# Sliding-window attention and a token mixer on one core: q and k in two-token rows, loads by four heads, mixing products with 128 columns, a new emission table

## The chip, the cores and the metric

The kernel runs on one core of a Trainium2 chip. Five engines matter: PE (TensorE, matrix products and transposes), ACT (ScalarE), DVE (VectorE), POOL (GpSimd, which here does little but issue the loads) and SP (SyncE, which issues the stores). Loads and stores themselves are moved by the core's 16 DMA engines. Results of PE go to PSUM, which has 8 banks; everything else lies in SBUF, with 128 partitions. The metric is the device time of one execution in microseconds (us), lower is better.

## The reference

Inputs are q, k and v of shape (8 batches, 8 heads, 576 tokens, 64), and three weights. Attention is causal within a window of 128 tokens, with a linear bias per head; its output, as rows of 512 numbers per token, goes into a mixer over the tokens of a batch.

```python
scores = scale * np.matmul(q, k.transpose(0, 1, 3, 2))      # scale 1/8
mask = (rel >= 0) & (rel < window)                           # rel = query - key, window 128
scores = np.where(mask, scores + bias[None], -1000000000.0)
attn = softmax(scores)
x = (attn @ v) as (batch, token, 512)
wq, wk = x @ w_q, x @ w_k                                    # 64 columns each
mixed = (1/8 * wq @ wk.T) @ x                                # per batch
out = np.maximum(mixed, 0.0) @ w_out
```

## The kernel before, in words

The kernel first makes a list of operations (`plan.op`), batch by batch, and then emits them in an order that is written out in the string `ORDER`. An entry such as `228P4+1` or `407G` means: operation 228 on PE with its result in PSUM bank 4, after 1 padding matmul on zeros; operation 407 on POOL. The letters are P for PE, A for ACT, D for DVE, G for POOL, S for SP. Every engine executes its own entries strictly in that order. An entry that has to wait holds all entries of the same engine behind it. The costs, due times and the `mode` that are passed to `plan.op` play no part in the emission; only the table does. `plan.run` (L117) checks that no operation stands ahead of one that it depends on. Before, the table has 773 entries, 279 of them on PE and 118 loads on POOL.

Per batch:

- **Loads** (`load`, L230, profile line L234; `load_qk` L237, `load_v` L266). All loads are issued by POOL and turn fp32 into fp16 on the way. Batches 0 and 1 take q and k in rows of six tokens (1536 B), two heads at a time, 192 rows per load (`ldsix`). Batches in `PAIRED` (2 and 3) take q and k in rows of two tokens (512 B), 1024 rows per load, that is 256 tokens of all eight heads. The others take rows of one token (256 B), 1024 rows for 128 tokens. v comes in rows of one token, 1024 rows per load (`ldv`); batch 0 takes it by heads, 512 rows per load. The last 64 tokens of each batch come in loads of their own (`ldqkt` into the tile `ntl`, `ldvt`), 512 rows on 64 partitions.
- **Buffers.** q and k lie in `natq` and `natk`, three buffers each (`NN`); v in `vn`, three (`NV`). So the loads of batch b wait until PE has transposed q and k of batch b-3, and used v of batch b-3.
- **Transposes of q and k** on PE (`q_transposes`): L378 for six-token rows, L407 for two-token rows (16 transposes of 128x64 per step), L418 for one-token rows (8 of 128x128), L435 for the last 64 tokens. Each step is copied to `qkT` by ACT (L222) or DVE (L224). For two-token rows the copy also puts the tokens back in order.
- **Attention** (`unit`, `values`): scores L483 in 64x64 tiles, exp on ACT (L496), the bias as a product with a table on DVE (L500), values L526 in 128x128 and 64x64 tiles, reciprocal and normalisation on DVE (L554, L555), transposes of the result L572.
- **Mixing** (`mixing`, `mix_one`, `outputs`): L608 (wk), L637 (wq), L650 (their product with x, `gm`), the mixing products L673 with the relu at L622 or L624, the output product L703 (four matmuls of 512 columns), a copy to `osb` and a store by SP (L710). There are 36 such output steps.

The mixing product is, before, four 64x64 matmuls of 288 columns per step j: two row halves c of `gm` and `wqT`, and two column halves y, each into its own 64 partitions of PSUM.

The order of loads on POOL is not batch by batch. The table mixes loads of up to three batches, and puts each load wherever its buffer is free and its use is not yet near.

Of the kernel before, what the change touches and what calls it, by code (L numbers as in the profile page):

```python
# [15 lines left out]
D = 64  # L16
H = 8
# [14 lines left out]
0G 1D 2A 4G 3D 5G 21D 31G 6D 32G 22A 20D 7D 33G 24A 34G 39G 40G 23D 12A 48P0+8 41G 14A 8A 50P1+2 42G 15A 51D 18A  # L32
43G 52P2+2 9A 16D 11A 35G 10D 17A 54P3+2 36G 49A 53D 55A 37G 64P4+3 19D 65A 38G 70P6 13D 67P0 44G 68A 66D 45G
71A 69D 46G 56P2+8 47G 73P4 72D 57A 58P3 25G 78P0 59D 74P 26G 60P6 75D 83P2 130G 61A 62P7 84A 131G 79P 132G 76P6
80D 63A 133G 77A 86P4+1 85D 89P2 138G 87A 81P7 139G 82D 90A 88D 140G 92P0+5 91D 143P6 141G 93P 144A 145P4 94D
142G 97P2 146A 98P 134G 159P6 99D 95P5 160A 135G 149P4 147P0 96D 136G 150A 100P1 148D 137G 101A 161D 162P2+2 27G
102P6 163A 28G 104P7 103D 164D 106P5 105A 29G 165P0 107A 108D 166A 30G 168P2 169P 109A 167D 231G 151P4 116P6
170D 114P0 152A 229G 153P5 115A 117D 171P4 154A 234G 155P2 172A 178P0 156D 110P6 230G 157P3 179A 173P4 158D 228G
111A 174P 112P0 180D 184P2 113A 235G 175D 232G 181P6+3 185A 121P0 233G 182A 127P1 186D 236G 122D 124P4 128A 183D
123S 176P5 129S 125A 187P2 238G 177D 243P6 126S 188P 320G 244A 192P0 189D 249P7 239G 247P4 250A 190P5 248D 193P  # L40
118P6 237G 194D 241P2 240G 119A 191D 195P3 242A 120S 318G 245P7 196D 246D 197P4 317G 251P0 198A 254P2 319G 252A
273P6 201P5 414G 255A 253D 332P4 324G 204D 199P0 274A 256D 323G 257P2 333D 202A 270P6 258A 407G 275D 271A
276P2+3 259D 322G 277A 260P6+2 272D 261P 203D 200A 265P2 278D 325G 205P4 207P0 262D 266P 206A 208A 328P4 267D
408G 326P5 329A 211P6 209P0 327D 284P2 212A 502G 330P4 210D 285P 331A 412G 263P6 286D 268P7 213P5 321G 264A 269A
287P0 405G 214A 340P2 288D 353P6 341A 215S 403G 337P4 334P0 354A 342D 225P2 409G 335A 355D 219P3 226D 338A 410G
279P6 216P0 336D 227S 220A 339D 404G 280P 221S 217A 356P4 281D 359P2 357A 218S 222P1 406G 360A 282P0 499G 358D
343P6 348P4 283D 415G 344P 361D 289P2 413G 345D 349P 290A 291P3 411G 350D 420P0 292A 293P2 416G 223D 421A 426P6
224S 294D 296A 295D 497G 428P7 427A 297P4 301P0 429D 299P2 302A 417G 346P6 300D 351P7 298A 367P0 352D 362P2 347A
419G 368P 363P 369D 303P4 422P7 418G 304A 364D 370P6 500G 311P4 371A 423D 507G 424P5 312A 305P0 589G 425D 313S
365P1 496G 306A 430P2 366D 511P6 431A 307S 498G 372P7 512D 449P4 503G 373A 432D 433P0 450A 452P2 376P6 501G 453A  # L50
374P7 451D 314P4 506G 377D 434A 454D 308P5 315D 594G 375A 379A 435D 513P2 316S 458P0 587G 309D 514A 459P 378D
310S 439P4 460D 504G 384P6 382P2 440P 385A 383D 461P0 508G 380P6 462D 386P2 381A 441D 436P0 586G 387A 509P6 437A
391P7 510D 505G 394P2 438D 392D 600G 515P3 395A 444P4 393S 516D 397P0 396S 597G 596G 536P6 398D 445P 537A 520P2
446D 595G 399S 605P1 521A 442P0 592G 606D 517P6 539P4 518A 538D 523P2 682G 447P1 522D 540A 542P6 519D 588G 543A
448D 455P4+2 541D 400P1 591G 456A 544D 526P6 401D 524A 593G 527P 457D 545P4 402S 388P1 601G 443A 528D 463P2 679G
389A 525D 546P 464P 390S 590G 547D 529P0 531P6 530A 607P1 690G 465D 532P 608A 548P4 598G 533D 466P5 603P0 599G
467A 550P2 549D 604A 534P1 468P6 602G 535D 551P 469A 684G 611P7 552D 472P5 612A 680G 470P4 473D 475A 474D 553P1
471A 683G 554A 478P2 482P6 476P4 479D 483A 555P0 686G 477D 609P1 556A 480P2 610D 559P6 687G 481D 616P4 681G 562A
632P0 617A 560D 613P2 561D 493P7 688G 633A 618D 619P4 494D 685G 614A 487P6 634D 495S 620A 635P0 689G 615D 638P2
557P7 488D 639A 691G 694P4 621D 489S 490P5 636A 640D 695D 627P2 558A 622P0 491A 637D 563P6 628P 492S 564A 698P4  # L60
629D 623P 699A 565P6 484P5 624D 566A 692P2 485A 641P0 693A 567P6 486S 642P 569P4 625P3 643D 570A 696P2 626A
646P4 697D 644P0 568A 647P 645D 703P2 648D 700P6 704A 574P1 701A 649P0 705D 577P4 575D 725P2 702D 578A 576S
706P6 571P5 726A 650D 579S 709P0 707A 727D 630P4 710P 722P2 631A 711D 719P6 723A 651P4 708D 712P0 720A 653P1
724D 714P2 652A 713D 733P6 572A 721D 715P 654A 573S 655P4 716D 734P 657A 728P0 656A 735D 717P5 658A 729P 718A
661P2 583P4 730D 662A 736P6 584A 731P7 737D 665P2 659P0 732D 585S 663P4 666A 580P6 660D 664A 738P7 581D 673P2
739A 582S 742P3 674A 740P0 675S 744D 745A 743A 670P1 741D 746P4 749P6 671A 755P2 748D 667P0 756A 757D 672S 747A
751A 752P2 750A 668D 676P1 753A 754A 669S 758P4 677A 767P5 678S 759A 761P6 760S 768D 764P7 762D 769S 770P0 763S
765A 766S 771A 772S
# [90 lines left out]
NN = 3  # L159
NV = 3  # L160
VHEADS = (0,)
PAIRED = (2,3)
# [5 lines left out]
def kernel(  # L168
# [10 lines left out]
    nc = tc.nc  # L179
# [57 lines left out]
    def load_qk(b):  # L237
        t0 = (b - 2.2) * PERIOD
        if b < 2:

            n = 2
            for h in range(0, H, n):
                for x, src in ((0, q), (1, k)):
                    load("ldsix", six[x][b][:, h : h + n, :], src[b, h : h + n].rearrange("h (p j) d -> p h (j d)", j=6),
                         96 * n, 1536, (-200 if b == 0 else -170) + (0 if h < 4 else 12) + h, [("six", x, b, y) for y in range(h // 2, (h + n) // 2)], slow=1.08)
# [12 lines left out]
        if b % 2 == 0:  # L258
# [106 lines left out]
    def q_transposes(b):  # L365
        p, i = b // 2, b % 2
        pb = p % 2
        if b < 2:
            for hp in range(4):
                for x in range(2):  # L370
# [3 lines left out]
                    def tr(e, x=x, hp=hp, g=g):  # L374

                        for j in range(6):
                            for a in range(2):
                                nc.tensor.transpose(ps16(g)[64 * a : 64 * a + 64, 96 * j : 96 * j + 96],  # L378
                                                    six[x][b][:, 2 * hp + a, D * j : D * j + D], idn[0:96, 0:96])

                    def ev(e, x=x, hp=hp, g=g):
# [3 lines left out]
                    plan.op("tsix", {"PE": 0.30}, tr, t0, ps_new=[g], mode="C", reads=["idn", ("six", x, b, hp)],  # L385
                            writes=[("sixed", x, b, hp)])
# [239 lines left out]
    def mix_one(b):  # L626
# [38 lines left out]
        for j in range(4):  # L665
            g4 = Ps(2, "other")

            def mm(e, j=j, g=g4):
                for c in range(2):
                    r = slice(64 * c, 64 * c + 64)  # L670
                    for y in range(2):
                        o = 256 * (j // 2 ^ c) + 128 * (j % 2) + 64 * y
                        nc.tensor.matmul(ps32(g)[64 * y : 64 * y + 64, 512 * c : 512 * c + 288],  # L673
                                         gm[i][r, o : o + 64], wqT[i][r, :], start=True, stop=True)

            tm = t0 + 3 + 0.5 * j
            plan.op("mx", {"PE": 0.125}, mm, tm, ps_new=[g4], mode="B", reads=[("gm", i, r) for r in (None, 0, 1)] + [("wqT", i)])
# [89 lines left out]
```

## Time and profile before

Three runs took 152.32, 154.08 and 154.88 us.

| What | us |
|---|---|
| median of the runs | 154.08 |
| the profiled execution's own time | 152.65 |
| its span | 150.9 |
| PE busy | 136.5 |
| DVE busy | 113.9 |
| ACT busy | 114.0 |
| POOL busy | 93.8 |
| last load issued / landed | 111.6 / 118.3 |
| last L703 matmul started, about | 146 |

An engine's busy time is the union of its instructions' spans. PE's matmuls overlap and their ends are modelled, so PE's busy time is not its work; the distance from the start of one step to the start of the next tells more. POOL's entries are the issues of loads; the transfer itself runs on the DMA engines later, and the view of DMA issues gives the time from issue to landing.

### The profile page before, as it was taken

To read this page: it belongs to the slowest core of one execution; us is meant where nothing else is said; L and a number is where in the kernel's file an instruction comes from. 1 tells how busy PE (TensorE), PEld (TensorE's weight loads), DVE (VectorE), ACT (ScalarE), POOL (GpSimd) and SP (SyncE) were. 2 spreads that over 40 slices of the span, in tenths; PEclk is the share of its full clock that TensorE was granted. 3 is DMA by queue.
4 is the path that set the end of the run, shared out by engine and by line. 5 is a ranking of instruction groups with operands and counts; after the bars stand their busy time and mean duration, and the time that the engine had idled before them with its cause. 6 is when DMAs were issued, how large, how long until landed. Compare 5 with 4: busy or idle time off the path is not lost.

```text
span 150.9 us, 6271 instructions
## 1 busy us (share of the span) xinstructions
PE 136.5 (91%) x2755; PEld 91.7 (61%) x2755; DVE 113.9 (76%) x221; ACT 114.0 (76%) x181; POOL 93.8 (62%) x123
## 2 busy tenths in 40 slices
PE   6989999799995896999999898997799999999990
PEld 2356677565783674577676656587656776866330
DVE  7497788687659995798868979895699697995430
ACT  7956968796579789859679649955879998885831
POOL 7999997599686668994999694959880000000000
PEclk9999999999999999999999999999999999999999
DMA  2999999999999999999999999999999313013365
GB/s 29 146 148 141 150 140 147 188 163 160 212 225 204 178 155 171 171 246 174 189 176 215 178 205 187 219 207 171 143 133 195 115 74 139 17 61 150 150 269 195
DMA packets 95674, 24.64 MB, mean 163 GB/s; under 512 B 87456, under 2 KB 91040, under 8 KB 95648
## 3 DMA queue, kind: packets, MB, share of 16 engines
q0 software_dynamic: 90464, 14.82, 142.3%
q1 hardware_dynamic: 5184, 9.44, 17.8%
q8 instruction: 21, 0.34, 1.0%
q14 instruction: 5, 0.04, 0.1%
HBM read 29.62 MB, written 9.44 MB: 259 GB/s over the span
## 4 chain that ended last, share of the span: by engine, by line
PE 48%; POOL 17%; DMA 11%; ACT 9%; DVE 7%; issue 5%; DVEq 0%; POOLq 0%; ACTq 0%
PE psb L703 17%; POOL vn L234 7%; PE psb L526 7%; DMA natk<-in_k_dram 6%; ACT pt L496 6%; DMA vn<-in_v_dram 5%; PE psb L483 5%; PE psb L418 4%; PE psb L572 4%; POOL natk L234 4%; POOL natq L234 4%; PE psb L608 3%; PE psb L673 2%; DVE x L555 2%; PE psb L637 2%
## 5 line engine op out<-in xcount | busy, mean ns | idle before, releaser
L496 ACT ACTIVATE pt<-psb 128x1024 f16<-128x1024 f32 x48 | 46.6, 1031 | 4.0 <-PE psb L483 3.6
L234 POOL DMA_DIRECT2D vn<-in_v_dram x44 | 36.6, 849 | 8.2 <-PE psb L572 2.1
L500 DVE TENSOR_TENSOR pt<-pt,bt 128x1024 f16<-128x1024 f16 x48 | 32.3, 686 | 6.7 <-ACT pt L496 6.4
L703 PE MATMUL psb<-wout,rm 128*128 128x512 f16 x144 | 35.5, 380 | 0.0
L526 PE MATMUL psb<-vn,pt 64*64 64x65 f16 (+1 forms) x832 | 27.9, 194 | 1.8 <-DMA vn<-in_v_dram 0.8
L526 PEld LDWEIGHTS <-pt 64*64 64x64 f16 (+1 forms) x832 | 23.3, 103 | 7.4 <-issue 2.9
L555 DVE TENSOR_TENSOR x<-psb,inv 128x640 f16<-128x640 f32 x32 | 26.4, 824 | 1.1
L222 ACT COPY qkT<-psb 128x1024 f16<-128x1024 f16 (+1 forms) x23 | 19.6, 850 | 7.9 <-PE psb L378 4.0
L234 POOL DMA_DIRECT2D natq<-in_q_dram x28 | 23.4, 843 | 3.2 <-DMA natq<-in_q_dram 1.6
L234 POOL DMA_DIRECT2D natk<-in_k_dram x28 | 23.4, 846 | 2.9 <-DMA natq<-in_q_dram 1.4
L703 PEld LDWEIGHTS <-rm 128*128 128x128 f16 x144 | 12.2, 98 | 13.1 <-issue 0.9
L222 ACT COPY osb<-psb 128x512 f32<-128x512 f32 x21 | 12.5, 595 | 9.2 <-PE psb L703 8.7
L483 PE MATMUL psb<-qkT 64*64 64x192 f16 (+2 forms) x672 | 17.3, 228 | 2.2 <-issue 1.3
L224 DVE COPY qkT<-psb 128x1024 f16<-128x1024 f16 (+1 forms) x20 | 15.8, 788 | 4.3 <-PE psb L378 2.4
L483 PEld LDWEIGHTS <-qkT 64*64 64x64 f16 x672 | 12.1, 106 | 8.6 <-issue 6.3
L622 ACT ACTIVATE rm<-psb 128x576 f16<-128x576 f32 (+1 forms) x26 | 14.5, 599 | 2.8 <-PE psb L673 2.7
L721 PE MATMUL psb<-wz 128*128 128x512 f16 x43 | 13.6, 438 | 2.6 <-ACT pt L496 1.4
L572 PE MATMUL psb<-idn,x 128*128 128x128 f16 x160 | 13.9, 220 | 1.2 <-DVE x L555 0.9
L224 DVE COPY osb<-psb 128x512 f32<-128x512 f32 x15 | 10.3, 688 | 4.6 <-PE psb L703 4.5
L572 PEld LDWEIGHTS <-x 128*128 128x128 f16 x160 | 9.5, 98 | 4.8 <-DVE x L555 2.7
L554 DVE RECIPROCAL inv<-psb 128x10 f32<-128x10 f32 x32 | 6.9, 217 | 6.1 <-PE psb L526 4.5
L222 ACT COPY xT<-psb 128x576 f16<-128x576 f16 x14 | 9.0, 652 | 1.8 <-PE psb L572 1.7
(64 smaller groups left out, 148.7 us busy)
## 6 DMA issues: line engine op xcount, KB each, us to landing
out_dram<-osb SPq DMA_DIRECT2D x36, 256.0 KB, 4.7
vn<-in_v_dram POOLq DMA_DIRECT2D x28, 128.0 KB, 7.4
natq<-in_q_dram POOLq DMA_DIRECT2D x16, 128.0 KB, 6.4
natk<-in_k_dram POOLq DMA_DIRECT2D x16, 128.0 KB, 7.0
natq<-in_q_dram POOLq DMA_DIRECT2D x8, 144.0 KB, 5.1
natk<-in_k_dram POOLq DMA_DIRECT2D x8, 144.0 KB, 5.4
vn<-in_v_dram POOLq DMA_DIRECT2D x16, 64.0 KB, 5.3
natk<-in_k_dram POOLq DMA_DIRECT2D x4, 256.0 KB, 7.4
```

The source lines that it names most:

```text
L222: nc.scalar.copy(o, i)
L224: nc.vector.tensor_copy(out=o, in_=i)
L234: plan.op(name, {eng: issue}, lambda e: e_.dma_start(out=dst, in_=src), prio, reads=reads, writes=writes, lat=-slow * n * max(17.5, w / 21 ...
L483: nc.tensor.matmul(ps32(g)[half : half + 64, o : o + hi - lo], qkT[pb][r, i, 1, hp, k0 : k0 + 64], qkT[pb][r, i, 0, hp, q0 + lo - c : q0 + ...
L496: nc.scalar.activation(out=cols(pt, 64), in_=ps32(g).rearrange("t (a s c) -> t a s c", a=2, s=2), func=AF.Exp, scale=SCALE)
L500: nc.vector.tensor_tensor(out=cols(pt, 64), in0=cols(pt, 64), in1=cols(bt[:, z], 0), op=ALU.mult)
L526: nc.tensor.matmul(ps32(gv)[lo:hi, o : o + D + 1], pt[klo:khi, a, y, c : c + m], vv[klo:khi, kb, 2 * hp + a, :], **flags)
L555: nc.vector.tensor_tensor(out=xs[b % NX][:, :, 128 * hp : 128 * hp + 128].rearrange("t j (a d) -> t a j d", a=2), in0=px[:, :, :, 0:D], in ...
L572: nc.tensor.transpose(ps16(g)[:, 128 * t : 128 * t + 128], xs[b % NX][:, t, 128 * hp : 128 * hp + 128], idn)
L622: nc.scalar.activation(out=o, in_=s, func=AF.Relu, scale=WSCALE)
L703: nc.tensor.matmul(ps32(g), rm[pb][:, db, o : o + 128], wout[:, db, :], start=(db == 0), stop=(db == 3))
L721: nc.tensor.matmul(psb[:, g.bank, :], wz[:, 0:P], wz[:, 0:512], start=True, stop=True)
```

## The change

Four things are edited, and the table is replaced by another that fits the new list of operations.

- `PAIRED` names batches 2 to 7 instead of 2 and 3: q and k of batches 4 to 7 come in two-token rows, are transposed by L407's code and copied by the reordering copy.
- Loads of q and k (two-token rows) and of v (batches 1 to 7) are split by heads: `QG` and `VG` are 4, so each load has 512 rows instead of 1024.
- The mixing product uses 128 columns of `gm` at once: two matmuls per step in 64x128 tiles instead of four in 64x64 tiles.
- `SIX` names the batches of six-token rows, which stay 0 and 1.
- `ORDER` has 809 entries, 279 of them on PE and 154 loads on POOL. Which of ACT and DVE makes a copy is part of the table, so that has changed too: for instance, 29 of the 36 output copies are on ACT instead of 21, and 21 of the 36 relu steps on DVE instead of 10.

```diff
 ORDER = """
-0G 1D 2A 4G 3D 5G 21D 31G 6D 32G 22A 20D 7D 33G 24A 34G 39G 40G 23D 12A 48P0+8 41G 14A 8A 50P1+2 42G 15A 51D 18A
...
+0G 1D 2A 4G 3D 5G 20D 31G 6D 22D 32G 23A 33G 24A 7D 34G 39G 40G 48P0+8 21D 41G 9A 8A 49D 50P1+2 42G 12A 51D 11A
...
 VHEADS = (0,)
-PAIRED = (2,3)
+SIX = (0, 1)
+PAIRED = (2, 3, 4, 5, 6, 7)
+QG, VG = 4, 4
...
                 if b in PAIRED:
-                    load("ldqk", nat[x][b % NN][:, c].rearrange("p (h e) -> p h e", e=128),
-                         src[b, :, 256 * c : 256 * c + 256, :].rearrange("h (p j) d -> p h (j d)", j=2),
-                         1024, 512, t0, [("nat", x, b % NN, c, y) for y in range(2)], reads=[("sixed", x, b % NN, y) for y in range(4)])
+                    for y in range(0, H, QG):
+                        load("ldqk", nat[x][b % NN][:, c].rearrange("p (h e) -> p h e", e=128)[:, y : y + QG],
+                             src[b, y : y + QG, 256 * c : 256 * c + 256, :].rearrange("h (p j) d -> p h (j d)", j=2),
+                             128 * QG, 512, t0, [("nat", x, b % NN, c, z // 4) for z in range(y, y + QG, 4)], reads=[("sixed", x, b % NN, y) for y in range(4)])
...
             for t in range(4):
-                load("ldv", vv[:, t, :, 0:D], v[b, :, 128 * t : 128 * t + 128, :].transpose([1, 0, 2]), 1024, 256, -164 + t if b == 1 else t0,
-                     [("vn", b % NV, t, h // 2, h % 2) for h in range(H)])
+                for y in range(0, H, VG):
+                    load("ldv", vv[:, t, y : y + VG, 0:D], v[b, y : y + VG, 128 * t : 128 * t + 128, :].transpose([1, 0, 2]),
+                         128 * VG, 256, -164 + t if b == 1 else t0, [("vn", b % NV, t, h // 2, h % 2) for h in range(y, y + VG)])
...
                 for c in range(2):
                     r = slice(64 * c, 64 * c + 64)
-                    for y in range(2):
-                        o = 256 * (j // 2 ^ c) + 128 * (j % 2) + 64 * y
-                        nc.tensor.matmul(ps32(g)[64 * y : 64 * y + 64, 512 * c : 512 * c + 288],
-                                         gm[i][r, o : o + 64], wqT[i][r, :], start=True, stop=True)
+                    o = 256 * (j // 2 ^ c) + 128 * (j % 2)
+                    nc.tensor.matmul(ps32(g)[:, 512 * c : 512 * c + 288], gm[i][r, o : o + 128], wqT[i][r, :],
+                                     start=True, stop=True)
```

The lines of the new table that the prediction speaks of hold, in POOL's order, the entries `331G` (k of batch 3), `529G` (the first load of v of batch 5, into the buffer that batch 2 used), `438G` (v of batch 4), `727G`, `724G`, `721G` (v of batch 7, into the buffer that batch 4 used), and at its end `717G`, `634G`, `629G`, `726G` (k of batch 7, v of batch 6 twice, v of batch 7).

More of the change, by code (lines that the diff above doesn't have):

```diff
@@ new lines @@
+143G 150A 151P0 94D 144G 97P4 152A 163P6 98P 145G 164A 95P1 99D 153P0 146G 96A 165D 134G 100P2 154A 135G 101D
+169P6 102P3 136G 170A 137G 104P4 103A 171D 166P0 27G 105A 106P5 167A 28G 109D 29G 108A 107D 155P2+3 168D 30G
+112P6 114P0 156A 116P4 232G 113D 157P3 117A 237G 115D 177P6 158A 172P4 251G 182P0 173P 183A 234G 159P2 174D 178P
+240G 161P3 160A 179D 110P0 162A 175P4 241G 176A 188P2 111D 332G 180P5 189A 185P6 184D 235G 127P4 181D 186A 243G
+190D 121P0 128A 242G 187D 118P1 129S 122A 233G 191P2 123S 329G 119A 196P6 192P 238G 120S 197P 193D 124P5 236G
@@ new lines @@
+198D 431G 194P4 125A 255P0 195A 245G 126S 199P1 256D 239G 257P2 200A 258A 246G 201P3 330G 203P5 202A 253P6 340G
+204A 205P7 254A 336G 259P4 208D 206A 252G 207A 260A 213P0+2 334G 209P2 215P6 214D 261P5 216A 248G 210D 211P0
+262A 247G 346P4+1 212A 249G 288P6 263P2 347A 335G 217P5 264A 250G 220P0 218D 424G 289A 265D 282P2 219S 285P4
+244G 221D 283A 229P1 342G 290D 222S 286A 269P6 284D 433G 266P2 352P0 270A 344G 287D 223P4 353D 333G 267A 226P5
+331G 230A 268D 291P6 338G 227A 296P2 231S 271D 292P 224A 228S 297P 423G 293D 277P0 225S 272P4 427G 278P 298D
@@ new lines @@
+721G 467D 471P1 565A 572D 551P4 619G 417P0 472D 546A 614G 566D 492P2 418D 631G 552A 494P3 547D 616G 419S 548P6
+493A 567P0 495D 549A 533G 496P4 553D 420P5 621G 497A 499D 568A 498D 618G 550D 500P2 506P6 635P4 421A 507D 620G
+501A 502P0 422S 636D 637P5 627G 503A 504P6 638A 625G 554P2 505D 559P0 720G 555P 569D 560P 508P4 628G 561D 712G
+573P6 509A 556D 643P5 713G 510S 562P0 639P1 644D 716G 557P4 574P 719G 641P2 563D 558D 632G 511P3 642A 640D 722G
+575D 578P4 512A 670P0 715G 579P 671A 513S 645P2 580D 711G 576P6 514P7 646A 723G 577D 581P0 672D 718G 515A 664P4
@@ new lines @@
+651P2 582D 665A 516S 648P6 714G 647D 583P1 725G 652A 666D 732P0 717G 728P4 584D 649A 733D 585P5 634G 587P2 729A
+629G 586D 667P6 589D 517P3 588A 726G 668A 590D 650D 593P0 591P4 518A 594D 597P6 730P2 598A 519S 653D 595P0 731A
+734P3 592D 654P6 735A 669D 655P 659P4 656D 596A 736P2 660P 737A 761P0 661D 657P6 602P7 762A 658D 673P2 738D 603A
+662P4 763D 674P 663A 604S 755P0 742P6 675D 756A 599P5 743A 676P4 757D 678P2 739P0 677D 679P 600D 740A 758P6
+605P4 744D 601S 759A 741D 611P5 680D 606A 745P0 612A 750P6 607S 760D 746P 613S 681P4 747D 769P2 682A 751P 770P
@@ L69 @@
+752D 748P5 683P4 749A 771D 764P0 684A 753P6 765P 754D 772P7 766D 687P5 773A 685P4 688A 689D 690A 767P2 686D
+608P3 768A 691P6 693P0 609A 695P4 692D 774P2 694A 610S 696D 697P6 775A 776P3 698A 778P0 777D 708P1 779A 780D
+781D 702P2 709A 710S 785P4 782P6 703A 791P0 787D 699P3 793A 786D 704S 792A 784D 788P4 783D 700A 705P2 790D 789D
+701S 806P0 706A 800P1 707S 807A 794P6 808S 801D 797P7 802S 795D 803P3 796S 798A 799S 804A 805S
 """
@@ L238, in load_qk @@
         t0 = (b - 2.2) * PERIOD
-        if b < 2:
+        if b in SIX:
             n = 2
@@ L243, in load_qk @@
                 for x, src in ((0, q), (1, k)):
-                    load("ldsix", six[x][b][:, h : h + n, :], src[b, h : h + n].rearrange("h (p j) d -> p h (j d)", j=6),
-                         96 * n, 1536, (-200 if b == 0 else -170) + (0 if h < 4 else 12) + h, [("six", x, b, y) for y in range(h // 2, (h + n) // 2)], slow=1.08)
+                    load("ldsix", six[x][b % NN][:, h : h + n, :], src[b, h : h + n].rearrange("h (p j) d -> p h (j d)", j=6),
+                         96 * n, 1536, (-200 if b == 0 else -170) + (0 if h < 4 else 12) + h if b < 2 else t0 + 0.1 * h, [("six", x, b % NN, y) for y in range(h // 2, (h + n) // 2)], slow=1.08,
+                         reads=[("sixed", x, b % NN, y) for y in range(h // 2, (h + n) // 2)] + [("natd", x, b % NN)])
             return
@@ L257, in load_qk @@
                          1024, 256, t0, [("nat", x, b % NN, c // 2, c % 2)], reads=[("sixed", x, b % NN, y) for y in range(4)])
-        if b % 2 == 0:
+        if b % 2 == 0 and (b not in SIX or b + 1 not in SIX):
             p = b // 2
@@ L367, in q_transposes @@
         pb = p % 2
-        if b < 2:
+        if b in SIX:
             for hp in range(4):
```

57 lines of the change are left out of this document (17 added, 40 removed).

## The prediction

> **What bounds the kernel now.** I read the page first, for which engines are full and when.
>
> ```profile
> span 150.9 us, 6271 instructions
> ...
> PE 136.5 (91%) x2755; PEld 91.7 (61%) x2755; DVE 113.9 (76%) x221; ACT 114.0 (76%) x181; POOL 93.8 (62%) x123
> ...
> POOL 7999997599686668994999694959880000000000
> PEclk9999999999999999999999999999999999999999
> DMA  2999999999999999999999999999999313013365
> ...
> q0 software_dynamic: 90464, 14.82, 142.3%
> ```
>
> Two stages show. Until slice 31 (about 117 us) the DMA engines are full; POOL, which only issues loads, is not. Afterwards no loads are left and PE carries the end. So I read those 34 us by windows, then the chain in order of time.
>
> ```profile
> 113.00:147.00 34.00, 33.90 (x592) 21.29 (x589) 24.86 (x46) 27.37 (x47) 0.00 (x0) 1.00 0.52 129
> ```
>
> ```profile
> 56.30 0.86 PE psb L703 x4
> ...
> 62.20 0.86 PE psb L703 x4
> ...
> 63.88 0.97 PE psb L703 x4
> ...
> 141.74 5.30 PE psb L703 x24
> 147.11 0.58 ACT osb L222
> ```
>
> PE is busy 33.90 of 34.00 us there, at full clock. The chain also gives PE's price of a step and of a change of array shape: four L703 matmuls take 0.86 us when a 128x128 step follows, 0.97 when a 64-row or 64-column step does. All steps show it (L526's value products 0.30 or 0.40, transposes at L572 0.28 or 0.38): a change of shape costs 0.10.
>
> With such prices I add up PE's 279 steps as the emission table lists them. Scores (L483) 0.24, values (L526) 0.305 and 0.25, L572 0.28, L608 0.59, L637 0.49, L650 0.57, L673 0.13, L703 0.86, L378 0.28, L407 0.47, L418 and L435 0.45, 0.22 per padding matmul, 0.10 per change of shape (140 of them): **126.8 us of work**. The last step ended at 146.0, so PE was 19.2 us behind its own work. That lag was 7 us after 20 steps, 13.1 after 100, 16.7 after 180, 19.1 after 200 and flat from there. The time is work plus lag plus 4.9 us for the last copies and stores; the profiled execution adds 1.75 (152.65 against a span of 150.9).
>
> Who makes the lag? Loads, partly:
>
> ```profile
> PE psb L572 <- DVE x L555: 0.9, 3, 0.4
> PE psb L673 <- DVE gm L224: 0.9, 1, 0.9
> PE psb L526 <- DMA vn<-in_v_dram: 0.8, 1, 0.8
> ...
> PE psb L407 <- DMA natk<-in_k_dram: 0.7, 1, 0.7
> ```
>
> Some waits end with a landing, all before 54 us; later ones end with ACT or DVE. But the order of steps is fixed around loads that come late. Hence the last two views, the issues with their time to landing, and POOL's timeline:
>
> ```profile
> vn<-in_v_dram POOLq DMA_DIRECT2D x28, 128.0 KB, 7.4
> ...
> vn<-in_v_dram POOLq DMA_DIRECT2D x16, 64.0 KB, 5.3
> ```
>
> ```profile
> 10.31 2.99 POOL L234 DMA_DIRECT2D vn<-in_v_dram  x4
> ...
> 60.27 3.54 POOL L234 DMA_DIRECT2D natk<-in_k_dram  x4
> ```
>
> A load of 512 rows on 128 partitions costs POOL 0.735 from start to start (2.99 for four, the last one 0.78), a load of 1024 rows 0.867. Landing takes 7.4 us where the DMA engines are backed up. The eight head loads of v in batch 0 (512 rows, engines not yet full) landed after 4.27 to 5.23, 4.65 on average.
>
> **The change, part by part.**
>
> *Two-token rows for batches 4 to 7.* The packet records of 52 to 56 us hold 4,260 rows of 256 B and 331 of 512 B, those of 48 to 52 us 469 and 2,480. That is about 0.95 us per 1,000 of the short and 1.43 per 1,000 of the long. Per batch 8,192 short rows (7.8 us) become 4,096 long ones (5.9): 1.9 us saved, 7.7 for four batches. Loads are 99 us of DMA work before and 91 after, plus 12 to 14 us of the stores that fall among them: the DMA engines could be done near 106 us instead of 118.3. PE: 16 transposes go from L418 (0.45) to L407's kind (0.47), +0.3. Their evictions cost ACT the same (1.01 both ways), DVE 1.22 instead of 0.69. With the table's new split, DVE goes from 123 us of work to 128, ACT stays at 124. Both lie beside PE; uncovered, 0.53 for each of the 8 on DVE, 4.2.
>
> *Loads by four heads.* 40 loads of q and k become 48 and 28 of v become 56, all of 512 rows: 104 x 0.735 = 76.4 where 68 x 0.867 = 59.0 stood. With the 50 other loads (33.6 before and after) and the first issue at 1.4, POOL needs **111.4 us without one wait**; before, it needed 94.0 and used 112.5, the rest being waits, mostly for landings. So POOL takes the DMA engines' place as the pacer. The price's bounds are 0.685 (512 rows on 64 partitions, the tail loads of batches 2 to 6) and 0.867 (1024 rows). I take 0.735, from loads of the same 128x4x64 shape.
>
> The Trainium skill ("DMA: Bandwidth & Descriptors", Anatomy of one DMA — SWDGE (gpsimd) path) speaks against this part: it calls descriptor generation small and says many descriptors can be emitted before the cost shows, so a half load would cost POOL nearly what a whole one does. The rows say 0.735 against 0.867: mostly fixed, as the page has it, but not all.
>
> *Mixing with 128 columns.* 128 matmuls of L673 become 64, in 64x128 tiles. The row is 0.12 us for four concurrent 64x64 matmuls of 288 columns. Two row halves of 128 columns take 0.12 if they run side by side, as the score products' row halves do, and 0.25 if not. I take 0.12: gain 0, and at worst 32 x 0.13 = 4.2 lost. The new shape joins three others in the queue.
>
> *New table.* SP's 36 stores stay as they are. Counted in the table, PE changes shape 158 times instead of 140 (+1.8), and has 41 padding matmuls instead of 43 (-0.4). PE's work becomes 126.8 + 0.3 + 1.8 - 0.4 = **128.5**.
>
> **The lag afterwards**, by landing time x and POOL's summed issue times, where a load meets its step:
>
> | Load (table entry) | POOL's sum | PE work ahead of its use |
> |---|---|---|
> | k of batch 3, 331G | 53.1 | 47.9 |
> | v of batch 5, 529G | 56.8 | its slot is free after 47.5 |
> | v of batch 4, 438G | 81.5 | 73.8 |
> | v of batch 7, 724G | 88.0 | its slot is free after 76.4 |
> | v of batch 6, 629G | 109.9 | 101.5 |
>
> The first gives a lag of 53.1 + x - 47.9 = 5.2 + x. 529G waits for PE (47.5 + lag) x - 4.1 longer than POOL's 56.8, and all loads behind it on POOL wait too: q and k of batches 3 and 4 first, whose transposes PE then waits for. 438G makes the lag 7.7 + x + (x - 4.1), 724G waits x - 3.9 more, and behind it stand q, k and v of batches 6 and 7. 629G makes the last lag 8.4 + x + (x - 4.1) + (x - 3.9) = 3x + 0.4. With x = 4.65: **14.35**. PE ends at 128.5 + 14.35 = 142.85 instead of 146.0, 3.15 earlier: 152.65 - 3.15 = 149.5. The profiled execution is among the fastest shown (median 154.08, 1.43 above), so I add half of that: **150.2**.
>
> **Rivals** (their times on the profiled execution's own scale).
>
> *POOL in a loop with PE (slower).* If loads keep landing as they do now, x is 7.0: the lag becomes 21.4, PE ends at 149.9, 3.9 later: 156.5. The waits at 529G and 724G are its place, each holding every load behind it; from x = 5.7 (a lag of 17.5) nothing is gained. For it: DMA work of about 104 us within 110 is still dense. Against: a waiting POOL lets the engines drain.
>
> *PE's own waits stay.* No wait of PE after 54 us ends with a landing, and the last q of batch 7 landed at 116.4 but was transposed only at 121.1. If lag comes from handing work to ACT and DVE, it stays 19.2, and the 1.7 us of added work counts: 154.4. DVE's 5 us more speak for it; against, the old order had those late loads built in.
>
> *A cheaper pacer.* At 0.685 per load POOL needs 106.2, and the same steps at x = 5 give a lag of about 11.5: 146.6. With x = 4.0 at 0.735 it is 12.4: 147.5.
>
> *Row halves that don't overlap:* 4.2 more, 153.7. *Half loads as dear as whole ones* (the page's account): 102 x 0.132 = 13.5 more ahead of 629G, so a lag near 27 and about 162; the 0.735 rows leave it little.
>
> **How the numbers follow.** Forecast 0.43; POOL loop 0.21; own waits 0.19; cheaper pacer 0.12; no overlap 0.03; dear halves 0.02. The lag moves 3 us with each us of landing, so the forecast alone reaches from 148 to 152.5. The range takes the cheaper pacer and most of the loop: 147 to 157. A measurement here tells about 2% from no change. Faster by more: just over half of the forecast and the cheaper pacer, with what a high run of before adds, 0.40; slower by more: the loop, dear halves and some of own waits, 0.27; between, 0.33.
>
> **What would show it.** Right: POOL's row in tenths near 9 until slice 29 or 30, half loads 0.73 apart and landing in 4.3 to 5.5 us, last L703 step near 143, L673 steps of two matmuls in 0.12 to 0.25. Wrong: POOL waits of several us on L526 with landings of 7 us (the loop); POOL done by 112 but PE's end still at 147 (own waits); L673 pairs of 0.25 and more with a step of their own shape next (no overlap).

## The result, and the profile after

The changed kernel takes **162.19 us** (median of four runs, 161.64 to 162.66), where the kernel before took 153.69 (152.32 to 154.88) beside it: a ratio of 1.058 [1.050, 1.067]. Forecast were 150.2, with 147 to 157 as the range. The profiled execution took 161.64, its span 159.8. Here and below, ratios and their 95% intervals leave out executions more than 1.5% above the fastest of their kernel, while medians and ranges are of all.

The first page, lines that answer to those of before:

```profile
span 159.8 us, 6424 instructions
...
PE 139.5 (87%) x2817; PEld 92.2 (58%) x2817; DVE 116.3 (73%) x228; ACT 113.8 (71%) x174; POOL 111.7 (70%) x159
...
POOL 7999989959849997889969996999799100000000
PEclk9999999999959999999999999999999999999999
DMA  2999999999999999999999999999999921501365
...
q0 software_dynamic: 74656, 14.82, 111.5%
```

POOL is busier by 17.9 us and issues loads until slice 31, at 4.0 us a slice. Its last load is issued at 123.5 us and lands at 128.9 (before: 111.6 and 118.3). The loads' packets need less time (111.5% of 159.8 us against 142.3% of 150.9), so the DMA engines were relieved as intended; they finish later because they get their work later.

PE's waits, and then POOL's, as engine, tile and line, what ended the wait, us in total, times, longest:

```profile
PE psb L413 <- DMA natk<-in_k_dram: 3.8, 4, 1.8
PE psb L413 <- DMA natq<-in_q_dram: 2.9, 4, 1.0
...
PE psb L532 <- DMA vn<-in_v_dram: 1.3, 2, 0.7
...
PE psb L441 <- DMA ntl<-in_q_dram: 1.2, 1, 1.2
```

```profile
POOL vn L237 <- PE psb L532: 3.8, 4, 1.4
POOL vn L237 <- PE psb L413: 2.1, 1, 2.1
POOL natk L237 <- issue: 1.8, 1, 1.8
POOL vn L237 <- DMA natq<-in_q_dram: 1.3, 2, 0.7
POOL vn L237 <- DMA vn<-in_v_dram: 0.9, 2, 0.7
```

Before, PE lost 1.5 us to landings in the lines shown and POOL waited long without harm. Now PE's transposes of two-token rows (L413) wait 6.7 us for q and k, most of it between 41 and 68 us, and again for k of batch 6 and q of batch 7 (1.76 at 110.1, 0.78 at 123.2). The lag, PE's distance behind its own work, was 9.2 us when 60 steps had started (8.3 before), 20.7 at 120 (13.5) and 27.4 at the end (20.1). So most of the difference came up between 39 and 77 us, and the later loads held it. With 1.7 us of added work that is 9.0 us, the difference of the spans (8.9).

In the chain of work that ended last, POOL stands where PE stood (start, length, what; xN merges N pieces):

```profile
60.48 7.28 DMA natq<-in_q_dram
...
91.18 5.25 DMA vn<-in_v_dram
...
117.23 5.94 DMA natq<-in_q_dram
...
150.73 5.30 PE psb L708 x24
```

From 48 to 123 us the chain runs mostly along POOL's issues, one behind the other, jumps to PE at a landing, and comes back to POOL where a load waits for a buffer. From 127.7 on PE runs to its end without a gap, as it did before in its last 34 us.

The mixing products kept their price. Three pairs of them, and one pair with a step of another shape behind it, in the same chain:

```profile
149.05 0.47 PE psb L678 x6
...
150.50 0.23 PE psb L678 x2
```

A pair takes 0.12 us, as four matmuls did, and the change of shape another 0.10.

**A limit that the prediction did not see.** POOL's timeline (start, length, line, transfer, xN; in brackets the idle time before, and what ended it by the profile):

```profile
38.70 1.57 POOL L237 DMA_DIRECT2D natq<-in_q_dram  x2
...
45.09 0.76 POOL L237 DMA_DIRECT2D natq<-in_q_dram  x1
47.99 0.74 POOL L237 DMA_DIRECT2D vn<-in_v_dram  x1 [2.14 <-PE psb L413]
```

The load at 47.99 goes into a v buffer that had been free since 16.7, so the PE step in the bracket is not what held it. Eight loads earlier POOL had issued 329G (the second of the two at 38.70, at 39.46), and that landed at 47.46. In every trace of this case the loads take eight semaphores in turn (a semaphore is a counter that tells of the landing), and most of them wait for their own one first: 138 of 154 here, 105 of 118 before. So a load is issued only when the eighth before it has landed. In all 17 profiles no load is issued earlier than 0.28 us after that landing; where it is the last thing to come, the distance is mostly 0.28 or 0.53. I call this the window of eight. It was there before, too. Two loads of the kernel before, issued 0.28 and 0.53 us after the eighth load before them had landed:

```profile
53.52 0.87 POOL L234 DMA_DIRECT2D natk<-in_k_dram  x1 [1.42 <-DMA natq<-in_q_dram]
54.88 0.87 POOL L234 DMA_DIRECT2D natq<-in_q_dram  x1 [0.49 <-DMA natq<-in_q_dram]
```

Counting to the window the waits that end within 1.2 us of that landing and after any buffer was free, POOL's 11.8 us of waits after the change are 6.2 for the window, 3.8 for v buffers (529G, 630G, 724G, 727G) and 1.8 at 33.76 us. Before they were 15.7 and 2.1. The wait at 33.76 ended 1.23 us after the eighth load before had landed, and so did a load near that time in five other kernels, after waits of 0.7 to 3.0 us. So it most likely hangs on the window as well, which makes 8.0; why the distance is 1.23 there stays open.

The window counts loads, not rows. With whole loads eight issues take 8 x 0.867 = 6.9 us, with halves 8 x 0.735 = 5.9; less 0.3, I estimate that a half load may land after at most 5.6 us without holding POOL. The 114 loads of this size land after 5.2 on average, but 40 of them take longer than 5.6. And eight half loads are half as many rows in flight.

### The profile page after: what moved, and what is told of

The parts are those of the page before. It is cut to its first block, busy times and chain, and to the rows that moved or that the text cites. A ratio compares the mean times of both kernels' runs of the same rounds, so it can differ in the third digit from the quotient of the medians.

```text
span 159.8 us, 6424 instructions
## 1 busy us (share of the span) xinstructions
PE 139.5 (87%) x2817; PEld 92.2 (58%) x2817; DVE 116.3 (73%) x228; ACT 113.8 (71%) x174; POOL 111.7 (70%) x159
## 3 DMA queue, kind: packets, MB, share of 16 engines
q0 software_dynamic: 74656, 14.82, 111.5%
q1 hardware_dynamic: 5184, 9.44, 16.7%
## 4 chain that ended last, share of the span: by engine, by line
POOL 37%; PE 30%; DMA 23%; issue 4%; ACT 2%; DVE 2%; POOLq 0%; ACTq 0%; DVEq 0%
POOL vn L237 18%; DMA natq<-in_q_dram 12%; PE psb L708 9%; POOL natq L237 8%; POOL natk L237 8%; PE psb L532 6%; DMA natk<-in_k_dram 4%; DMA ntl<-in_q_dram 4%; DMA vn<-in_v_dram 3%; PE psb L413 3%; PE psb L489 2%; PE psb L578 2%; POOL ntl L237 2%; PE psb L643 2%; PE psb L614 2%
## 5 line engine op out<-in xcount | busy, mean ns | idle before, releaser
L237 POOL DMA_DIRECT2D vn<-in_v_dram x72 | 55.2, 796 | 9.0 <-PE psb L532 3.8
L225 ACT COPY qkT<-psb 128x1024 f16<-128x1024 f16 (+1 forms) x28 | 24.3, 880 | 15.5 <-PE psb L413 9.5
L532 PE MATMUL psb<-vn,pt 64*64 64x65 f16 (+1 forms) x832 | 25.8, 193 | 1.9 <-DMA vn<-in_v_dram 1.3
L237 POOL DMA_DIRECT2D natk<-in_k_dram x32 | 24.4, 768 | 2.3 <-issue 1.8
L225 ACT COPY osb<-psb 128x512 f32<-128x512 f32 x29 | 17.0, 592 | 12.4 <-PE psb L708 9.5
L532 PEld LDWEIGHTS <-pt 64*64 64x64 f16 (+1 forms) x832 | 22.2, 103 | 6.1 <-issue 1.9
L237 POOL DMA_DIRECT2D natq<-in_q_dram x32 | 24.6, 781 | 0.6 <-DMA natq<-in_q_dram 0.2
L630 DVE TENSOR_SCALAR rm<-psb 128x576 f16<-128x576 f32 (+1 forms) x21 | 13.2, 666 | 4.9 <-PE psb L678 4.8
L489 PEld LDWEIGHTS <-qkT 64*64 64x64 f16 x672 | 12.2, 106 | 5.9 <-issue 2.9
L227 DVE CAST gm<-psb 64x256 f16<-64x256 f32 (+1 forms) x14 | 5.9, 421 | 8.8 <-PE psb L656 5.7
L225 ACT COPY xT<-psb 128x576 f16<-128x576 f16 x12 | 7.7, 641 | 5.0 <-PE psb L578 5.0
```

What stands on the lines that cost most here:

```text
L225: nc.scalar.copy(o, i)
L227: nc.vector.tensor_copy(out=o, in_=i)
L237: plan.op(name, {eng: issue}, lambda e: e_.dma_start(out=dst, in_=src), prio, reads=reads, writes=writes, lat=-slow * n * max(17.5, w / 21 ...
L489: nc.tensor.matmul(ps32(g)[half : half + 64, o : o + hi - lo], qkT[pb][r, i, 1, hp, k0 : k0 + 64], qkT[pb][r, i, 0, hp, q0 + lo - c : q0 + ...
L532: nc.tensor.matmul(ps32(gv)[lo:hi, o : o + D + 1], pt[klo:khi, a, y, c : c + m], vv[klo:khi, kb, 2 * hp + a, :], **flags)
L630: nc.vector.tensor_scalar(out=o, in0=s, scalar1=WSCALE, scalar2=0.0, op0=ALU.mult, op1=ALU.max)
```

## The experiments

"Lag" is PE's lag at the start of its last step, with the prediction's prices of steps. Three theories: **pace** (POOL's issue time and window: it has nothing to spare now), **order** (where the loads stand in the table), **edits** (one of the other parts did it). Where a diff is set against the kernel before, that is the kernel before written with the change's parameters. Where loads are joined or cut, the table is renumbered and has an entry for each load; the diffs leave that out.

**Which part does it?** Whole loads with the changed kernel's table, halves with the old table (at the whole loads' places), two-token rows alone, 128-column mixing alone.

```diff
-QG, VG = 4, 4
+QG, VG = 8, 8
```

> The kernel after, with QG = VG = 8: q, k and v in loads of 1024 rows again, each at the place of its first half in the table (or the first legal place behind it); two-token rows, mixing with 128 columns and PE's order stay. POOL's issues sum to 80.0 us instead of 111.4. Theory pacer (POOL's 36 added issues and its waits set the pace): 150 to 155 us, POOL done by 110, PE's lag back under 20. Rival table (the new order of PE's steps, with 18 more changes of shape, is slow by itself): 158 us or more, although POOL is idle for a third of its time.

The changed kernel with whole loads: 161.33 us, ratio to before 1.049 [1.036, 1.063]. POOL's last load was issued at 112.9, but the lag was still 27.1. Another cause takes over: PE stops in the middle of steps with nothing to wait for (4.7 us in all, the lines "issue" of its waits), and then runs at half clock for 6.8 us (below, under hardware). Between 62 and 82 us the lag goes from 13.0 to 22.1 (in the same steps before, from 13.1 to 13.7); two stops of 1.75 and 2.00 us and the half clock, worth up to 3.4, make 7.2 of this. POOL waits 20.8 us for v buffers in this run, but that isn't what holds PE: none of PE's waits from 58 to 112 us ends with a landing.

```diff
-QG, VG = 8, 8
+QG, VG = 4, 4
```

> The kernel before, with only its v loads and its two-token q, k loads (batches 2 and 3) cut in two by heads, both halves at the whole one's place in the table. POOL's issues sum to 115.6 us instead of 93.9, the rows moved are the same. Theory pacer: 158 us or more, last load issued after 122. Rival table: within 2 us of before, 151 to 156, the DMA engines being as full as they were.

The kernel before with half loads: 161.06 us (159.27 to 162.49, where 153.56 ran beside it). Its largest waits of PE:

```profile
PE psb L424 <- DMA natq<-in_q_dram: 2.5, 2, 1.4
PE psb L532 <- DMA vn<-in_v_dram: 1.7, 1, 1.7
```

Last load at 124.6, lag 27.2. Halves alone give the kernel before the lag that the whole change had.

```diff
-PAIRED = (2, 3)
+PAIRED = (2, 3, 4, 5, 6, 7)
```

> The kernel before, with q and k of batches 4 to 7 in two-token rows of whole 1024-row loads, each at the place of the first of the two loads that it replaces. 7.7 us of DMA work fewer, POOL's issues 80.0 us; PE 11 changes of shape more and 16 dearer transposing steps (PE's work 128.2 instead of 126.8); 9 of the 16 reordering copies on DVE at 1.22 instead of 0.69 us. If loads make PE's lag: 147 to 150 us. If PE's lag is its own waits on ACT and DVE: 154 to 157 us.

Two-token rows in whole loads, alone: 160.39 us, 1.044 [1.031, 1.057]. The loads' packets fell to 118.7% of the span, and yet the lag was 25.9: PE stopped for 5.9 us with nothing to wait for (2.1 before), and for 3.4 us it ran at half clock. The saving in DMA work, by itself, bought nothing.

```diff
-                    for y in range(2):
-                        o = 256 * (j // 2 ^ c) + 128 * (j % 2) + 64 * y
-                        nc.tensor.matmul(ps32(g)[64 * y : 64 * y + 64, 512 * c : 512 * c + 288],
-                                         gm[i][r, o : o + 64], wqT[i][r, :], start=True, stop=True)
+                    o = 256 * (j // 2 ^ c) + 128 * (j % 2)
+                    nc.tensor.matmul(ps32(g)[:, 512 * c : 512 * c + 288], gm[i][r, o : o + 128], wqT[i][r, :],
+                                     start=True, stop=True)
```

> The kernel before with only the mixing product changed to two matmuls of 128 columns. PE changes shape 152 times instead of 140 in before's order, at 0.10 us: 1.2 us more work. If the two row halves run side by side (0.12 us a step): 152.5 to 155 us. If not (0.25 us): 157 to 158.5 us.

156.25 us (153.27 to 157.27) where 153.56 ran beside it: the runs lie too far apart to tell. The reverse, the changed kernel with four 64x64 matmuls:

> The kernel after with only the mixing product back to four 64x64 matmuls. PE changes shape 157 times instead of 158; 128 matmuls and weight loads more. If the mixing edit is neutral, as its steps of 0.12 us side by side say: within 1.5 us of the kernel after, 160 to 163. If it costs: 158 or less.

161.63 us, 1.056 [1.031, 1.082]: not to be told from 162.19. The mixing edit shows no effect, though this interval would hide one of some 4 us; that it is neutral rests on the price of its steps, 0.12 us a pair.

**Which loads?** Whole v loads with half q and k loads, in the changed kernel and on the kernel before; and whole loads with half of v left out in batches 3 to 7.

```diff
-QG, VG = 4, 4
+QG, VG = 4, 8
```

> The kernel after, with only v in loads of 1024 rows again (q and k stay in 512 rows of 512 B). POOL's issues sum to 94.5 us, near the 93.9 of before; no load is over 0.97 us of DMA work. Theory two sides (half loads make POOL late, whole two-token loads make PE's instruction stream late): both are eased, 150 to 155 us, PE waits for landings under 3 us in all, PE's stops inside a step under 2 us. If the table is slow by itself: 158 us or more.

164.25 us, 1.077 [1.058, 1.096]: worse, with less to issue. Each whole v load stands where its first half stood, ahead of q and k that PE wants sooner; PE waits 9.5 us for q and k, and POOL 14.7 us for v buffers. I put it down to order: the same loads in order of first use take 157.01 (below).

```diff
-PAIRED = (2, 3)
-QG, VG = 8, 8
+PAIRED = (2, 3, 4, 5, 6, 7)
+QG, VG = 4, 8
```

> The kernel before, with q and k of batches 4 to 7 in two-token rows, all two-token rows in 512-row loads, v whole, before's order of steps. POOL's issues 94.5 us, 7.7 us of DMA work less than before, PE's work 128.2. Theory two sides: 151 to 155 us, with less stopping inside steps than the 5.6 us of the same kernel with whole two-token loads (158.1 us span). If the two-token rows cost by PE's added work and the DVE copies: 157 us or more again.

The kernel before with two-token rows in half loads, v whole: 155.90 us, 1.024 [1.007, 1.041]. POOL's sum is 94.5 us as before, its last load is issued at 111.2, PE's stops with nothing to wait for fall from 5.9 us to 0.2, the lag is 22.2. So half loads cure what whole two-token loads bring, as long as POOL can pay for them.

```diff
-                    load("ldv", vv[:, t, y : y + VG, 0:D], v[b, y : y + VG, 128 * t : 128 * t + 128, :].transpose([1, 0, 2]),
+                    n = VG if b < 3 else VG // 2
+                    load("ldv", vv[:, t, y : y + n, 0:D], v[b, y : y + n, 128 * t : 128 * t + 128, :].transpose([1, 0, 2]),
```

> The kernel after with whole loads, but v of batches 3 to 7 is loaded for heads 0 to 3 only (512 rows instead of 1024; heads 4 to 7 keep the numbers of three batches before, so that part of the result is left out). 10 us of DMA work fewer, POOL's issues 77 us, PE unchanged. If PE stops inside steps because its instructions come through DMA engines that are backed up with loads: the stops after 50 us fall from 5.8 us to under 2, no stretch of 6.8 us at half clock, 149 to 154 us. If they come from the program itself: the same stops, 158 us or more.

The changed kernel with whole loads, in which v of heads 4 to 7 of batches 3 to 7 isn't loaded: 154.27 us, 1.013 [0.996, 1.029], lag 20.3, 1.6 us of stops instead of 4.7 (the expectation's 5.8 draws the line a little differently). With fewer rows to move, the changed table costs about its 1.7 us of added work, as far as the interval tells.

**POOL's time by itself.** Both kernels got nearly the same extra work on POOL, with no load added or moved: iotas (instructions that fill a tile with counting numbers) on a scratch tile behind each v load of batches 1 to 7, two behind a whole one, one behind a half one.

```diff
...
-        plan.op(name, {eng: issue}, lambda e: e_.dma_start(out=dst, in_=src),
+        def go(e):
+            e_.dma_start(out=dst, in_=src)
+            for _ in range(2 if name == "ldv" else 0):
+                nc.gpsimd.iota(scratch, pattern=[[1, 256]], base=0, channel_multiplier=-1)
...
+        plan.op(name, {eng: issue}, go,
...
```

> The kernel before, with two iotas on a scratch tile behind each v load of batches 1 to 7: about 18 us more work for POOL, hence a sum near 112 as in the changed kernel, but its loads, their 1024 rows and their order as before. Theory 'issue time alone': POOL's end goes late as it does in the changed kernel, the last load is issued near 120 and the time is 158 to 162. Rival 'rows in flight': with 1024 rows a load, the window of eight holds enough to keep the DMA engines full, POOL's 15.7 us of waits for the window shrink by what it works more, the last load is issued at 112 to 116 and the time is 153 to 156.

The kernel before: 154.40 us, 1.007 [1.001, 1.012]. Its group of iotas and POOL's row on the page:

```profile
POOL 7999999987999999993899999999999600000000
...
L238 POOL IOTA scratch<- 128x256 int32 x56 | 20.1, 359 | 2.0
```

Each theory had half of it. POOL's waits fell by 12.2 us (17.8 to 5.6), not by all of the added work; the last load went out at 119.6 instead of 111.6; and it cost 1.0 us (0.1 to 1.9 by the interval), since those loads had time to spare. DVE and ACT were as busy as before (113.6 and 114.0 us), so the iotas took time from POOL alone. Among the last 14 loads, the nearest first use stood 3.8 us after its landing before, and 1.5 now.

> The changed kernel with one iota on a scratch tile behind each of its 56 half v loads: about 20 us more work for POOL, as much as two iotas behind each of the 28 whole v loads added to the kernel before (20.1 us there, for 1.0 us of time). Theory 'POOL's pace': the changed kernel has no slack left on POOL, its waits of 11.8 us take up 6 to 8 us of it, the last load is issued 12 or more later (at 135 or after) and the time rises by 9 to 13, to 171 to 175. Rival 'order alone': the waits of PE come from where the loads stand and not from POOL's pace, the time rises as little as it did for the kernel before, to 162 to 165.

The changed kernel: 170.03 us, 1.102 [1.091, 1.113], so 7.8 us above 162.19 for 17.7 us more of POOL's busy time. Its row, and PE's first waits:

```profile
POOL 7999999929989999799999999999999900000000
```

```profile
PE psb L419 <- DMA natq<-in_q_dram: 8.4, 6, 2.8
PE psb L390 <- DMA natk<-in_k_dram: 3.6, 3, 2.3
```

The last load went from 123.5 to 133.6, the lag from 27.4 to 36.6. The changed kernel has nothing to spare on POOL: there, the nearest first use among the last 14 loads stood 0.04 us after its landing without the iotas already. The forecast of 171 to 175 was a little high. In these five kernels the last load's issue less PE's lag is nearly the same: 96.1 (changed kernel), 96.1 (four v buffers, below), 97.0 (changed kernel with iotas), 97.4 (before with halves), 97.3 (before with iotas). The kernel before stands at 91.5. So where POOL is late, PE follows it nearly one for one, as far as these five show; in another order of loads the number is another (104.2 in order of first use, below).

**Order and buffers.**

```diff
-NV = 3
+NV = 4
```

> The changed kernel with four v buffers instead of three: POOL's 3.8 us of waits for a free v buffer (at 529G, 630G, 724G, 727G of the table) go, nothing else changes. Theory 'window': the loads then wait for the eighth load before them instead, the time stays at 160.5 to 162.5. Rival 'buffers': the wait is taken out of POOL's path, and the time falls by as much, 157.5 to 159.5.

159.12 us, 1.027 [1.020, 1.033]: 3.1 below the changed kernel. (One more operation fills the new buffer's constant columns.) The waits for v buffers are gone, those for the window rose from 6.2 to 8.5, the last load went out at 121.4, and the lag is 25.3. The rival was right: most of those 3.8 us stood in the path that sets the time.

The next two only move loads of batches 2 to 7 in the table, into the order in which PE first uses them; 529G, which waited for its buffer, then stands behind 394P to 541P.

```diff
-273P 426G 350P6 529G 274D 348P7 351A 299P2 337G 294P3 279D 349A 275P4 439G 444P5 295D 300A 430G 276D 376P0 445D
...
+322S 393D 394P1 617G 396P4 458A 395D 541P5 478D 616G 398A 323P0 399D 542A 529G 397D 459D 528G 404P2 402P6 324A
...
```

> The changed kernel with the same loads, but those of batches 2 to 7 stand on POOL in the order in which PE first uses them (in the table they are spread, with v of batches 5, 6 and 7 early, where three of them wait for a buffer). POOL's sum of issue times stays 111.4 us. Theory 'POOL's pace' (its issue time, and the window of eight loads in flight): the last load is still issued at 119 to 124, the time is 158 to 162. Rival 'order' (loads put where they wait for buffers or come before a load that PE wants sooner): the 3.8 us of buffer waits go, and most of the 6.5 us of PE's waits for landings between 43 and 70 us, the time is 153 to 156.

The changed kernel: 158.14 us, 1.021 [1.013, 1.030], 4.0 below it. Its lag is 22.7 although the last load goes out at 126.9, later than in the changed kernel (123.5), because the last nine loads are now v of batch 7, wanted last (3.5 to 7.6 us after landing). No wait for a buffer is left, but 14.2 us of waits for the window. The first uses within 0.3 us of their landing fall from 26 to 14 loads (before: 11).

> The kernel before with only its loads of batches 2 to 7 put on POOL in the order of PE's first use (POOL's sum 93.9 as before). Theory 'order': order of first use is simply the better order, for the kernel before too, 150 to 153. Rival 'order and pace': the kernel before has slack on POOL, so order is worth nothing to it or costs some by bunching q, k of a batch: 154 to 158.

The kernel before in the same order: 158.64 us, 1.030 [1.020, 1.039], so it loses what the other gained. Its whole loads stand bunched: landing takes 6.9 us on average (6.6 before), POOL waits 19.2 us for the window, and PE stops for 5.3 us in all with nothing to wait for. Order of first use isn't better in itself; it suits half loads.

**A version of what was good.** Whole v loads, half q and k loads, order of first use, with the changed table and with the old one.

> The changed kernel with whole v loads (1024 rows) and half q, k loads, the loads of batches 2 to 7 in order of PE's first use: POOL's sum is 94.5 us instead of 111.4, as before the change. Theory 'POOL's pace': with 17 us less to issue POOL is no longer behind, the last load is issued near 110, the time is 152 to 156 (PE's work is 128.5, the lag back near 20). Rival 'whole loads crowd the DMA engines': PE stops in the middle of steps and waits for q, k behind whole v loads, as with whole v loads at the places of the first halves (164), the time is 158 to 164.

157.01 us (153.05 to 159.77), where 154.35 ran beside it. In the profiled execution (157.36) PE stops for 5.6 us with nothing to wait for, and runs at half clock for 6.8: the rival's sign.

> The kernel before with two-token rows in 512-row loads for q, k of batches 2 to 7, whole v loads, and the loads of batches 2 to 7 in order of PE's first use: POOL's sum is 94.5 us, PE's work 128.2, DMA rows as few as in the changed kernel. With the loads at their old places it was 155.9. Theory 'order': as with the changed kernel, order of first use gives back 3 to 4 us, 152 to 153, level with the kernel before or a little faster. Rival 'whole v loads crowd the engines': PE's instructions and q, k come late behind bunched whole loads, 155 to 159.

156.05 us (153.13 to 157.21), where 154.27 ran beside it: no gain on 155.90 at the old places that could be told. POOL is done by 113.4 and 110.9 in these two, so POOL no longer paces them, but PE's added work (1.7 and 1.4 us) remains. No version beat the kernel before.

**What stays open.** Of the 8.5 us, 4.0 come back by order, and 3.1 by a fourth v buffer. The two weren't run together; since no wait for a buffer is left in the new order, they most likely overlap. What is left at 158.14 fits the 1.7 us of PE's work and a lag 2.6 us longer, of which a stretch at half clock makes 1.7 (3.4 us at half speed); that split is argued, not shown. The window itself wasn't widened, since the number of semaphores isn't set in these kernels, so its share is known from its waits alone.

## Why the prediction was wrong

- **PE's work of 128.5** held: with the prediction's prices the lag drifts by 0.3 us over the last 58 steps. Row halves do run side by side.
- **The end of before was read 0.9 us short.** At 146.0 the last step started; it ended at 147.0. Counted as the forecast counts, the lag of before was 20.1 at the end, not 19.2, and not flat after 200 steps (19.1). This moves the forecast by 0.9 us to the fast side and explains nothing of the miss.
- **POOL's pace of 0.735** held: half loads go out 0.73 to 0.74 apart. The rival drawn from the Trainium skill's account ("DMA: Bandwidth & Descriptors", Anatomy of one DMA — SWDGE (gpsimd) path), which calls descriptor generation small, gave a time near the measured one by luck: it has a half load as dear as a whole one, and the rows contradict that price here.
- **That POOL would become the pacer** held, and so did the last equation. 629G, the last v load on which PE's time hangs, was issued at 122.77 and landed 5.68 us later; less the 101.5 us of work ahead of its use this gives a lag of 26.95, and PE began that step 0.08 us after the landing.
- **The failed step is the sum of POOL's waits: 1.3 us forecast, 11.8 measured.** The prediction put 629G's issue at 111.2 (109.9 and 1.3). It came 11.6 later, and with 1.0 more of landing that is the whole way from a lag of 14.35 to 26.95. Of the two waits counted, 529G took 0.86 and 724G 1.13. Not counted were 630G and 727G, which refill v buffers in the same way (1.76), the window of eight (6.2), and the wait at 33.76 us (1.8), most likely the window's too.
- **The reason behind that step was wrong.** The prediction did read POOL's waits of before as waits for landings, but had nothing left of them once the DMA engines are relieved. They were waits for the eighth load before, 15.7 of 17.8 us. Halving the loads makes eight of them issue 1.0 us sooner, and the time to landing falls by only 1.5 us on average (6.64 to 5.17), so that the window goes on holding POOL.
- **The first gap** stood in the same step: 331G was to go out at 53.1 and went out at 58.9, after 3.6 us of waits for the window and the 1.8 at 33.76, none for a v buffer. It landed 6.30 us later instead of 4.65, PE began its step 0.04 us after that, and the lag was 17.4 where the forecast had 9.85. From 60 to 120 steps the lag grew by 11.5 us where it had grown by 5.3.
- **Rivals.** "POOL in a loop with PE" named the right engine, the right places and the right sign, but priced only landings of 7 us at two waits (156.5). "PE's own waits stay" fell: landings returned as PE's largest waits. "A cheaper pacer" fell with the 0.735.
- **The 1.9 us per batch saved by two-token rows** shows in the packets' time, if not as that number (142.3% to 118.7% of the span), and is worth nothing here: alone, in whole loads, the rows made the kernel 6.8 us slower.

## What to carry to other kernels

Before cutting transfers into smaller ones, count how many may be in flight: if the limit is a number of transfers, cutting them in two halves the rows in flight and shortens the time that each may take to land (issue time times that number), so that the issuing engine's waits need not go. Price a pacer's sum with these waits in it, and test its slack directly by giving the issuing engine idle work: 1.0 us for the kernel before and 7.8 for the changed one said more than any share of busy time. The size of loads and their order in a hand-written table belong together; a better order for one size was a worse one for the other.

## What the runs showed of the hardware

**PE can stop inside a step with nothing to wait for.** From PE's timeline of the changed kernel with whole loads:

```profile
62.43 0.25 PE L410 MATMUL psb<-idn,natq 128*64 128x128 f16 x2
64.42 0.58 PE L410 MATMUL psb<-idn,natq 128*64 128x128 f16 x14 [1.75 <-issue]
...
68.70 0.73 PE L653 MATMUL psb<-x,wkn 128*64 128x256 f16 x9
71.44 0.30 PE L653 MATMUL psb<-x,wkn 128*64 128x256 f16 x1 [2.00 <-issue]
```

In the 17 profiles of this case all 20 stops of PE over 0.5 us that nothing in the profile ended came to their end 1.3 to 1.9 us after the end of a 16,384-byte packet of the queue that the profile's page calls "instruction" (21 or 22 packets per execution). They add up to 4.7 us with whole two-token loads in the changed table, 5.9 in the old one, 2.1 in the kernel before, 1.6 in the changed table with half of v left out, and none in the changed kernel. I read this as PE's instructions coming late where loads crowd the DMA engines. The Trainium skill ("Runtime: NRT & Kernel Launch", Instruction fetch mechanics) has instructions refilled in 16 KiB blocks, the cost mostly hidden. The packets agree; hidden it isn't here, with 2.5 us at one stop (the kernel before in order of first use). That late packets cause the stops is read from their times: no run changed them alone, and the packets themselves take no longer where PE stops, mostly about 1 us in both kernels.

**The granted clock halves after a window in which PE was busy for about half the time or less.** Windows of the changed kernel (window, length, busy us and instructions of PE, PEld, DVE, ACT, POOL, then PE's clock, DMA share, GB/s):

```profile
40.35:43.78 3.43, 1.62 (x27) 1.07 (x26) 2.15 (x3) 1.77 (x3) 3.00 (x5) 1.00 1.51 236
43.78:47.20 3.42, 3.38 (x44) 3.05 (x46) 0.00 (x0) 1.58 (x3) 2.07 (x3) 0.50 1.56 199
```

In the traces' clock records half-clock stretches inside the span last 3.41 or 6.83 us. I laid a grid of 3.413 us through them in all 17 profiles: all 20 windows with PE busy below 1.8 us were followed by half clock, one of eight between 1.8 and 1.96, and none of the some 700 above that, as far as they ran at full clock. None of the 20 was idle, the least had 0.55 us of work. The Trainium skill ("TensorE: Matmul & The Clock Gate", Part 1) says that the clock drops after an idle window of about 3.4 us. The length agrees; idle it need not be here, up to some 1.8 us of work in it is too little. Waits of 1.5 to 2 us in one window can so cost PE another 1.7 us, as they did at 43.8 us in the changed kernel, though not in the kernel before, whose least window has 2.1 us of work. In the changed kernel the time itself hardly hangs on these 1.7 us: PE waited for landings again at 48.9, 57.6, 60.9 and up to 67.8 us, and no load waited for what PE did in that stretch.
